# One PSUM pool of single banks, other first loads, and a new order table in an attention-then-FFN kernel

## The chip, the cores and the metric

One core of a Trainium2 chip runs the kernel: TensorE (PE; its weight loads are a row of their own, PEld), VectorE (DVE), ScalarE (ACT), GpSimd (POOL) and SyncE (SP), with 16 DMA engines between the core's SBUF and HBM. PSUM, which PE writes and DVE and ACT read, has eight banks of 128 x 512 float32. The metric is the device time of one execution in microseconds (us); several executions are timed, and their median counts.

## The reference

```
proj = x @ w_phi                                   # q and k: 8 batches, 8 heads, 576 x 64; w_phi 64 x 128
proj = proj - max|proj| over its 128 features
phi  = [exp(proj), exp(-proj)]                     # 256 features
kv = phi(k)^T v;  z = sum over tokens of phi(k)    # per batch and head
attn = phi(q) kv / (phi(q) z + 1e-6)
x = attn, heads side by side                       # 4608 tokens x 512
out = relu(x @ w_in)^2 @ w_out                     # 512 -> 2048 -> 512
```

## The kernel before

The 4608 tokens are 36 tiles of 128. A batch gives two parts of two tiles each and a rest of 64 tokens; the rests of two batches share a tile. The FFN takes the tiles in chunks: four chunks of one tile, then sixteen of two.

**Keys** (`k_batch`). For batches 0 and 1 PE transposes the keys (`e_tp`, line 630) and a copy brings them to SBUF as `kT`; from batch 2 on a DMA transpose does it (`XB_IN` = 2). Then, in five groups, PE multiplies by `w_phi` (`e_kp`, line 660; matmuls on 64 rows, two at a time on the two halves of the array) into a `pj` tile of two PSUM banks. DVE reduces the tile to the largest magnitude per token (`e_red`, line 595, 128x1024), ACT takes exp of +proj and of -proj (`e_exp`, line 602, 128x1024 twice). ACT makes exp of the maxima (`em`, line 704), DVE scales the values by it (`e_va`, line 755; `e_vr`, line 738, for the rest), and PE sums keys times values (`e_kv`, lines 776 and 781, 65 columns a matmul) into what a copy stores as `kvs`.

**Queries** (`q_batch`). Likewise transposed; PE projects twice, with tokens on partitions for the maxima (`e_qm`, line 878) and with features on partitions for the exps (`e_qp`, line 888); DVE reduces (line 925), ACT takes exps (line 915). For each tile PE multiplies the two sign halves with `kvs` (`e_nd`, line 970; line 978 for rests, on half of the columns), DVE scales and adds them (`e_t`, lines 1009 and 1013, 128x520), divides (`e_rd`, `e_xo`, lines 1032 and 1042) and gives the x tile `xo`. For batches 0 and 1 PE transposes `xo` (`e_xtp`, line 1083) and a copy stores `xT`; from batch 2 on (`XB_X` = 2) SP does it by a DMA transpose (lines 1065 and 1068).

**FFN.** `hp_chunk`: 16 matmuls fill one `mo` bank (line 1133), relu to `hr` (lines 1151 on ACT, 1153 on DVE), square into `h` (1161 on ACT, 1163 on DVE, 128x512 each). `op_chunk`: 16 matmuls of 512 columns sum a tile's output in one `mo` bank (line 1189), a copy and an SP DMA bring it out.

**PSUM.** Six banks are three `pj` tiles of two; two banks are `mo`, for transposes, the FFN and batch 0's `kv`.

**Start.** PE runs 24 matmuls on zeros (`e_first`), then waits for the identity that POOL makes after it has issued the loads of half of batch 0's keys and of its values. The other half of the keys comes by SP as float32 and is cast. `WARM` adds idle matmuls ahead of some PE steps, and `e_fill` 40 more in the head. `w2` holds `w_phi` for the two array halves, zeros elsewhere.

**Order.** Every step is an `Op` with the engines that it may run on; the program adds 1718 of them in a fixed sequence, and the table `ORDER` lists their numbers in the order in which they are issued, a minus sign choosing the second engine. Each engine runs its own in that order and waits by semaphores for what it needs. Steps that use the 64-row or half-column form of the array are marked (`mode`), the others use all of it. POOL and SP issue DMAs from their queues, and an issue whose buffer is still in use blocks what is behind it.

Of the kernel before, what the change touches and what calls it, by code (L numbers as in the profile page):

```python
# [8 lines left out]
F32 = mybir.dt.float32  # L9
# [94 lines left out]
)  # L104


WARM = {44: 7, 54: 10, 58: 6, 62: 2, 74: 13, 93: 4, 117: 5, 139: 2, 149: 8}


class Slots:  # L110
# [54 lines left out]
class Plan:  # L165
# [13 lines left out]
    def add(self, key, engines, emit=None, deps=(), take=(), give=(), after=(), locks=(), port=False, mode="full"):  # L179
        op = Op(key, engines, emit, deps, take, give, after, locks, port, mode)  # L180
        self.ops.append(op)
        return op

    def order(self):
        assert sorted(abs(n) for n in ORDER) == list(range(len(self.ops)))
        for n in ORDER:
            o = self.ops[abs(n)]
            assert not o.left
# [1079 lines left out]
```

## Time and profile before

| | |
|---|---|
| median of the runs | 360.28 us (359.89 to 363.01) |
| profiled execution, first to last instruction | 358.4 us |
| the median less that span | 1.9 us |
| first FFN matmul in it | 28.41 us |
| last matmul's end in it | 354.8 us |
| mean granted TensorE clock | 0.990 |

The profile has busy times by engine and by stretches of time, groups of instructions (count, busy us, mean ns of one, idle time ahead of them), a chain of waits that ended last, a timeline (start, duration, instruction, in brackets what ended the idle time) and DMA issues. The profiled execution's own time is taken as its span and the 1.9 us around it.

### The profile page before, as it was taken

To read this page: it belongs to the slowest core of one execution; us is meant where nothing else is said; L and a number is where in the kernel's file an instruction comes from. 1 tells how busy PE (TensorE), PEld (TensorE's weight loads), DVE (VectorE), ACT (ScalarE), POOL (GpSimd) and SP (SyncE) were. 2 spreads that over 40 slices of the span, in tenths; PEclk is the share of its full clock that TensorE was granted. 3 is DMA by queue.
4 is the path that set the end of the run, shared out by engine and by line. 5 is a ranking of instruction groups with operands and counts; after the bars stand their busy time and mean duration, and the time that the engine had idled before them with its cause. 6 is when DMAs were issued, how large, how long until landed. Compare 5 with 4: busy or idle time off the path is not lost.

```text
span 358.4 us, 9254 instructions
## 1 busy us (share of the span) xinstructions
PE 346.4 (97%) x3860; PEld 239.1 (67%) x3894; DVE 292.4 (82%) x529; ACT 262.9 (73%) x436; POOL 58.5 (16%) x88
## 2 busy tenths in 40 slices
PE   8699999999999999999999999999999999999995
PEld 4378667775776676767576757757685768576754
DVE  5979998889998998788988699979988988591310
ACT  4979997996798774698849883798879867544641
POOL 8643323442160113100220002000000000000000
PEclk9969999999999999999999999999999999999999
DMA  9999999999997499607982194435203001113011
GB/s 161 185 197 207 194 208 141 170 181 187 186 152 138 83 171 150 107 15 145 124 126 53 59 149 96 61 89 82 60 16 88 18 35 48 65 34 88 2 59 59
DMA packets 92281, 39.33 MB, mean 110 GB/s; under 512 B 59728, under 2 KB 87760, under 8 KB 92240
## 3 DMA queue, kind: packets, MB, share of 16 engines
q0 software_dynamic: 42752, 18.09, 42.7%
q1 hardware_dynamic: 49328, 20.59, 28.6%
q8 instruction: 30, 0.49, 0.6%
q10 hardware_dynamic: 160, 0.07, 0.1%
q14 instruction: 11, 0.09, 0.1%
HBM read 36.77 MB, written 9.44 MB: 129 GB/s over the span
## 4 chain that ended last, share of the span: by engine, by line
PE 82%; DVE 8%; ACT 7%; issue 1%; POOL 1%; ACTq 0%; POOLq 0%
PE mo L1133 32%; PE mo L1189 31%; PE pj L781 4%; PE pj L970 4%; ACT kph L602 4%; PE pj L878 3%; PE pj L888 2%; DVE m L595 2%; PE pj L660 2%; DVE tmp L1009 1%; ACT hr L1151 1%; PE pj L776 1%; PE mo L781 1%; DVE va L755 1%; DVE hr L1153 1%
## 5 line engine op out<-in xcount | busy, mean ns | idle before, releaser
L1133 PE MATMUL mo<-xT,win 128*128 128x256 bf16 (+1 forms) x1280 | 139.3, 262 | 0.8 <-ACT hr L1151 0.2
L1189 PE MATMUL mo<-wout,h 128*128 128x512 bf16 (+1 forms) x558 | 131.2, 373 | 1.8 <-issue 0.2
L1133 PEld LDWEIGHTS <-win 128*128 128x128 bf16 x1280 | 111.3, 98 | 19.7 <-issue 4.3
L1189 PEld LDWEIGHTS <-h 128*128 128x128 bf16 x592 | 54.5, 98 | 57.3 <-issue 2.8
L915 ACT ACTIVATE qph<-pj 128x1024 bf16<-128x1024 f32 (+1 forms) x80 | 72.8, 940 | 11.6 <-PE pj L888 11.6
L1151 ACT ACTIVATE hr<-mo 128x512 bf16<-128x512 f32 x99 | 58.7, 598 | 28.2 <-PE mo L1133 27.0
L602 ACT ACTIVATE kph<-pj 128x1024 bf16<-128x1024 f32 (+1 forms) x80 | 71.2, 949 | 6.4 <-PE pj L660 4.9
L1163 DVE TENSOR_TENSOR h<-hr 128x512 bf16<-128x512 bf16 x82 | 33.7, 419 | 22.6 <-ACT hr L1151 22.0
L925 DVE TENSOR_REDUCE mq<-pj 128x8 f32<-128x1024 f32 (+1 forms) x40 | 44.2, 1108 | 4.5 <-PE pj L878 4.4
L595 DVE TENSOR_REDUCE m<-pj 128x8 f32<-128x1024 f32 (+1 forms) x40 | 44.3, 1111 | 3.4 <-ACT kph L602 1.7
L1161 ACT ACTIVATE h<-hr 128x512 bf16<-128x512 bf16 x62 | 38.9, 631 | 8.3 <-DVE hr L1153 7.5
L755 DVE TENSOR_TENSOR va<-vin,em 128x512 bf16<-128x512 bf16 x63 | 40.2, 683 | 0.1
L1153 DVE TENSOR_SCALAR hr<-mo 128x512 bf16<-128x512 f32 x45 | 30.6, 684 | 7.9 <-PE mo L1133 7.4
L417 ACT ACTIVATE ot<-mo 128x512 f32<-128x512 f32 (+1 forms) x24 | 14.0, 585 | 25.1 <-PE mo L1189 25.1
L1009 DVE TENSOR_TENSOR tmp<-pj,e 128x520 f32<-128x520 f32 x31 | 21.1, 692 | 6.1 <-PE pj L970 6.1
L970 PEld LDWEIGHTS <-qph 128*128 128x128 bf16 x512 | 21.9, 98 | 5.4 <-issue 1.5
L1042 DVE TENSOR_TENSOR xo<-tmp,rden 128x512 bf16<-128x512 f32 (+1 forms) x39 | 24.3, 631 | 0.5
L970 PE MATMUL pj<-kvs,qph 128*128 128x65 bf16 x512 | 24.4, 194 | 0.2
L781 PEld LDWEIGHTS <-kph 128*128 128x128 bf16 x512 | 21.5, 101 | 0.3
L1013 DVE TENSOR_TENSOR tmp<-pj,tmp 128x520 f32<-128x520 f32 x31 | 21.2, 692 | 0.5 <-PE pj L970 0.4
L781 PE MATMUL pj<-va,kph 128*128 128x65 bf16 x448 | 18.4, 194 | 0.0
L467 POOL DMA_DIRECT2D vin<-in_v_dram x8 | 7.2, 895 | 68.5 <-DVE va L755 63.1
(75 smaller groups left out, 268.5 us busy)
## 6 DMA issues: line engine op xcount, KB each, us to landing
out_dram<-ot SPq DMA_DIRECT2D x31, 256.0 KB, 2.4
vin<-in_v_dram POOLq DMA_DIRECT2D x8, 512.0 KB, 9.0
kin<-in_k_dram POOLq DMA_DIRECT2D x7, 512.0 KB, 11.9
qin<-in_q_dram POOLq DMA_DIRECT2D x7, 512.0 KB, 10.3
win<-in_moe_w_in_dram POOLq DMA_DIRECT2D x4, 512.0 KB, 10.1
wout<-in_moe_w_out_dram POOLq DMA_DIRECT2D x2, 1024.0 KB, 14.8
out_dram<-ot SPq DMA_DIRECT2D x10, 128.0 KB, 2.4
xT<-xo SPq DMA_TRANSPOSE x36, 2.6
```

The source lines that it names most:

```text
L595: nc.vector.tensor_reduce(out=st["m"].rearrange("p (n c) -> p c n", c=2)[:, :, n0 : n0 + n], in_=st["pj", g][:, :, :n], axis=AX.X, op=ALU. ...
L602: nc.scalar.activation(out=st["kph"][:, s, n0 : n0 + n].rearrange("p n c f -> p c n f"), in_=st["pj", g][:, :, :n], func=ACT.Exp, scale=1. ...
L755: nc.vector.tensor_tensor(out=st["va"][:, s, gs, 0:D], in0=tiles["v", b].rearrange("p h i d -> p (h i) d")[:, gs, :], in1=st["em"][:, s, g ...
L781: nc.tensor.matmul(out=kv[:, sum_of(h) - 2 * prs[0], :], lhsT=st["kph"][:, s, 2 * h + i // 2, i % 2, :], rhs=st["va"][:, s, h * NI + i, :] ...
L915: nc.scalar.activation(out=st["qph", pt][:, s, half, n0 : n0 + n], in_=in_, func=ACT.Exp, scale=1.0 - 2.0 * s)
L925: nc.vector.tensor_reduce(out=st["mq", pt][:, half, n0 : n0 + n], in_=in_, axis=AX.X, op=ALU.max, apply_absolute_value=True)
L970: nc.tensor.matmul(out=nps[:, n + 4 * (ab or 0), :], lhsT=qph[:, s, half, sl, :], rhs=kvs[:, s, sum_of(sl), :], start=True, stop=True)
L1133: nc.tensor.matmul(out=hp[:, mi, :], lhsT=win[:, kc, mc * P : (mc + 1) * P], rhs=st_x[c][:, kc, 0:nt, :], start=kc == kcs[0] and (ab is No ...
L1151: nc.scalar.activation(out=out_, in_=in_, func=ACT.Relu)
L1153: nc.vector.tensor_scalar(out=out_, in0=in_, scalar1=0.0, scalar2=None, op0=ALU.max)
L1161: nc.scalar.activation(out=out_, in_=hr, func=ACT.Square)
L1189: nc.tensor.matmul(out=st["op"], lhsT=hst["h2"][:, mc, tt * P : (tt + 1) * P], rhs=wout[:, mc, cols], start=(mc == 0), stop=(mc == KC2 - 1))
```

## The change

PSUM is one ring of eight single banks (`r_ps`). A step that had a two-bank tile takes two banks, each held and given back by itself; so the reduces and exps are two instructions of half the size, numerators come in two steps of four heads, each with two DVE instructions of half the size, and `kv` in two steps of two head pairs for all batches. The lock that keeps DVE and ACT apart on one projection of keys holds per bank. `e_qm` and `e_qp` are separate steps for all batches.

Relu results of two FFN banks lie in one `hr` tile, and one square handles both, except in the last chunk.

Batch 0: SP also loads the rest of the keys, and the values, as float32 in two halves; the rest is cast, the value products read float32. POOL makes the identity first. `w_phi` comes in one transfer to both halves; the zeroing of `w2` is gone. `e_fill` is gone.

POOL may run value products, rest products and `xo`. Only the two x tiles of batch 0's first part go through PE; the other eight of batches 0 and 1 go by SP's DMA transposes. From batch 3 on, the loads of a batch stand behind a small POOL copy that reads an `xo` of two batches earlier. The order table and `WARM` are new: 2084 steps, PE's among them 604 for 502, 47 value and 9 rest products and 21 `xo` with a minus sign (POOL).

```diff
-    XB_IN, XB_X = 2, 2
+    XB_IN, PE_X = 2, [(0, 0, 0), (0, 0, 1)]
...
-    r_pj = Ring("pj", 3, [P, 2, 4, P], F32, pool=ps)
-    r_mo = Ring("mo", 2, [P, 4, P], F32, pool=ps)
+    r_ps = Ring("ps", 8, [P, 4, P], F32, pool=ps)
-    r_hr = Ring("hr", 4, [P, 512], BF16)
+    r_hr = Ring("hr", 3, [P, 2, 512], BF16)
...
-            red_ops[g] = add(key, {"dve": dve(256 * n)}, e_red, [o_kp], give=[(r_pj.slots, hold)], locks=[lock])
+            for par in range(2):
+                lock = Lock()
...
+                red_ops.setdefault(g, []).append(add(key, {"dve": dve(128 * n)}, e_red, [o_kp],
+                                                     give=[(r_ps.slots, holds[par])], locks=[lock]))
...
-            o_fill = fill[0] = add(kd - 5.0, {"pe": (FILL * 0.0565, FILL * 0.0565 + 0.165)}, e_fill, [o_id], [r_mo.slots],
...
-            va_on = {"dve": (0.6, 0.69)}
+            va_on = {"dve": (0.6, 0.69), "pool": (1.0, 1.05)}
...
-                    if b >= XB_X:
+                    if (b, pt, half) not in PE_X:
...
+    def load_gate(b, key):
+        o_xo, owner, st, name = firsts[b - 2]
+
+        def emit(_):
+            nc.gpsimd.tensor_copy(out=mark[:, b : b + 1], in_=st[name][:, 0, 0:1])
```

More of the change, by code (lines that the diff above doesn't have):

```diff
@@ L369, in c_w2 @@
     def c_w2(op):
-        for half in range(2):
-            rows = slice(half * Dh, (half + 1) * Dh)
-            copy(op, w2[rows, half], wst[rows])
+        copy(op, w2, wst)
     def c_wst(_):
-        for half in range(2):
-            nc.scalar.dma_start(out=wst[half * Dh : (half + 1) * Dh], in_=w_phi)
+        nc.scalar.dma_start(out=wst, in_=w_phi.unsqueeze(0).to_broadcast([2, Dh, Fd]))
     def c_var(_):
@@ L417, in copy @@
             nc.scalar.activation(out=out_, in_=in_, func=ACT.Copy)
+        elif op.engine == "pool":
+            nc.gpsimd.tensor_copy(out=out_, in_=in_)
         else:
@@ L453, in load_first_k, with emit_r, e_rcast, emit_v @@
                 casts[g].append(add(-90, either(256), e_cast, [d], give=[(r_h2.slots, o_st)], after=[o_table, o_in]))
-        return casts
-    first_v = []
+        def emit_r(op):
+            st["r"] = r_ot.tile(op, [P, NP, D], [None, 2 * NP, D])
+            for h2 in range(2):
+                nc.sync.dma_start(out=st["r"][h2 * J : (h2 + 1) * J],
+                                  in_=k[0, :, SM:S, :].rearrange("(h2 pr) j d -> h2 j pr d", h2=2)[h2])
+        o_r, d_r = plan.issue("hw", 2, -98, {"sp": (1.0, 1.0)}, emit_r, "krf", (), [r_ot.slots], after=[o])
+        def e_rcast(op):
+            tiles["kr", 0] = r_rest["k"].tile(op)
+            copy(op, tiles["kr", 0], st["r"])
+        o_rc = add(-89, either(256), e_rcast, [d_r], [r_rest["k"].slots], [(r_ot.slots, o_r)], after=[o_table])
+        casts[4] = [o_rc]
+        d_v, o_v, o = [], None, o_r
+        for n in range(2):
+            def emit_v(op, n=n):
+                if n == 0:
+                    tiles["v", 0] = r_h2.tile(op, [P, H, NI, D], dtype=F32)
+                nc.sync.dma_start(out=tiles["v", 0].rearrange("p h i d -> p h (i d)")[:, 4 * n : 4 * n + 4],
+                                  in_=v[0, 4 * n : 4 * n + 4, 0:SM, :].rearrange("h (p i) d -> p h (i d)", i=NI))
+            o, d = plan.issue("hw", 1, -97, {"sp": (0.5, 0.5)}, emit_v, "vf", (), [] if o_v else [r_h2.slots], after=[o])
+            o_v = o_v or o
+            d_v.append(d)
+        return casts, o_rc, o_v, d_v
     def load(name, b, key, after=None):
@@ L481, in main @@
         def main(last):
[L482 removed]
+            return plan.issue("sw", 1, key, {"pool": (0.92, 0.95)}, emit_main, "main", (), [r_in[name].slots],
                               after=[prior, last])
@@ L575, in through_xbar @@
         return x1, t1, t2
-    kv_ops, gate, fill = {}, {}, {}
-    FILL = 40
+    kv_ops, gate = {}, {}
     def k_batch(b):
@@ L640, in e_cp @@
                     copy(op, st["kT"][:, n0 : n0 + n], st["ps", g][:, :n])
-                o_cp = add(key - 1.5, bf_copy(128 * n), e_cp, [o_tp], give=[(r_mo.slots, o_tp)])
+                o_cp = add(key - 1.5, bf_copy(128 * n), e_cp, [o_tp], give=[(r_ps.slots, o_tp)])
             cp_ops[g] = o_cp
         o_kp = None
-        for gs in [[g] for g in groups]:
-            key = kd - 6.0 - 2.2 * (4 - gs[0])
-            holds = {g: Hold(r_pj.slots) for g in gs}
-            def e_kp(op, gs=gs, holds=holds):
-                if gs[0] == 0:
-                    st["kph"], st["m"] = r_kph.tile(op), r_m.tile(op)
-                for g in gs:
-                    n0, n = GROUPS[g]
-                    pj = st["pj", g] = r_pj.tile(holds[g])
-                    warm(pj[:, 0], op.warm if g == gs[0] else 0)
-                    for u in range(n):
-                        for par in range(2):
-                            rows = slice(par * Dh, (par + 1) * Dh)
-                            nc.tensor.matmul(out=pj[:, par, u, :], lhsT=st["kT"][rows, n0 + u, :],
-                                             rhs=w2[rows, par, :], start=True, stop=True)
-            o_kp = add(key - 1, {"pe": mm(P, sum(GROUPS[g][1] for g in gs))}, e_kp,
-                       [cp_ops[g] for g in gs] + [o_w2],
-                       list(holds.values()) + ([r_kph.slots, r_m.slots] if gs[0] == 0 else []),
@@ new lines, in k_batch, with e_kp @@
+        for g in groups:
+            key = kd - 6.0 - 2.2 * (4 - g)
+            holds = [Hold(r_ps.slots) for _ in range(2)]
+            def e_kp(op, g=g, holds=holds):
+                if g == 0:
+                    st["kph"], st["m"] = r_kph.tile(op), r_m.tile(op)
+                n0, n = GROUPS[g]
+                pj = [r_ps.tile(hold) for hold in holds]
+                st["pj", g, 0], st["pj", g, 1] = pj
+                warm(pj[0], op.warm)
+                for u in range(n):
+                    for par in range(2):
+                        rows = slice(par * Dh, (par + 1) * Dh)
+                        nc.tensor.matmul(out=pj[par][:, u, :], lhsT=st["kT"][rows, n0 + u, :], rhs=w2[rows, :],
+                                         start=True, stop=True)
+            o_kp = add(key - 1, {"pe": mm(P, GROUPS[g][1])}, e_kp, [cp_ops[g], o_w2],
+                       holds + ([r_kph.slots, r_m.slots] if g == 0 else []),
@@ L666, in k_batch @@
                        give=[(r_kT.slots, o_kT)], after=[o_k0], mode="row")
             o_k0 = o_k0 or o_kp
[L668 to L679 removed]
+            after_kp(g, o_kp, holds)
@@ L866, in q_batch @@
                 key = xk - 9.0 + (12 if split else 1) * pi
-                hm, hq = Hold(r_pj.slots), Hold(r_pj.slots)
-                size = 256 * w
+                hm, hq = ([Hold(r_ps.slots) for _ in range(2)] for _ in range(2))
+                banks = [(half, 4 * bank, 4) if split else (bank, n0, n) for bank in range(2)]
                 def e_qm(op, pt=pt, pi=pi, mms=mms, w=w, hm=hm):
-                    pj = st["pm", pt, pi] = r_pj.tile(hm)
+                    pj = st["pm", pt, pi] = [r_ps.tile(hold) for hold in hm]
                     if pi == 0:
                         st["mq", pt] = r_mq.tile(op)
-                    warm(pj[:, 0], op.warm)
+                    warm(pj[0], op.warm)
                     for u in range(w):
@@ L877, in e_qm @@
                             rows = slice(par * Dh, (par + 1) * Dh)
-                            nc.tensor.matmul(out=pj[:, bank, u, :], lhsT=q_blocks(st, pt, blk + u, 1)[rows, 0],
-                                             rhs=w2[rows, par, :], start=True, stop=True)
+                            nc.tensor.matmul(out=pj[bank][:, u, :], lhsT=q_blocks(st, pt, blk + u, 1)[rows, 0],
+                                             rhs=w2[rows, :], start=True, stop=True)
                 def e_qp(op, pt=pt, pi=pi, mms=mms, w=w, hq=hq):
-                    pj = st["pq", pt, pi] = r_pj.tile(hq)
+                    pj = st["pq", pt, pi] = [r_ps.tile(hold) for hold in hq]
@@ L907, in q_batch @@
-                if split and pi:
-                    late = o_qm, o_qp
-                o_mq, o_q0 = o_mq or o_qm, o_q0 or o_qp
-                for s in range(2):
-                    def e_exp(op, pt=pt, pi=pi, half=half, n0=n0, n=n, w=w, s=s):
-                        in_ = st["pq", pt, pi][:, :, :w]
-                        if n == 8:
-                            in_ = in_.rearrange("p a b t -> p (a b) t")
-                        nc.scalar.activation(out=st["qph", pt][:, s, half, n0 : n0 + n], in_=in_, func=ACT.Exp,
-                                             scale=1.0 - 2.0 * s)
-                    exps.setdefault(pi, []).append(add(key + 2.5 + 0.2 * s, {"act": act(size)}, e_exp, [o_qp],
-                                                       give=[(r_pj.slots, hq)]))
@@ L921, in e_red @@
-                def e_red(op, pt=pt, pi=pi, half=half, n0=n0, n=n, w=w):
-                    in_ = st["pm", pt, pi][:, :, :w]
-                    if n == 8:
-                        in_ = in_.rearrange("p a b t -> p (a b) t")
-                    nc.vector.tensor_reduce(out=st["mq", pt][:, half, n0 : n0 + n], in_=in_, axis=AX.X, op=ALU.max,
-                                            apply_absolute_value=True)
-                reds.append(add(key + (3.5 if b == 0 else 0.5), {"dve": dve(size)}, e_red, [o_qm], give=[(r_pj.slots, hm)]))
+                o_qm = add(key, {"pe": mm(P, w * (1 + split))}, e_qm, need + [o_w2], hm + first[:1], give=qT_give,
+                           after=[o_mq], mode="row")
@@ new lines, in q_batch, with e_exp, e_red @@
+                o_qp = add(key + (0.1 if b else 2), {"pe": mm(128 * w, 1 + split)}, e_qp, need + [o_w2], hq + first[1:],
+                           give=qT_give, after=[o_q0], mode="row")
+                o_mq, o_q0 = o_mq or o_qm, o_q0 or o_qp
+                mine = []
+                for bank, (half_, h0, nh_) in enumerate(banks):
+                    for s in range(2):
+                        def e_exp(op, pt=pt, pi=pi, bank=bank, half_=half_, h0=h0, nh_=nh_, w=w, s=s):
+                            nc.scalar.activation(out=st["qph", pt][:, s, half_, h0 : h0 + nh_],
+                                                 in_=st["pq", pt, pi][bank][:, :w], func=ACT.Exp, scale=1.0 - 2.0 * s)
+                        exps[half_, h0, s] = add(key + 2.5 + 0.2 * s, {"act": act(128 * w)}, e_exp, [o_qp],
+                                                 give=[(r_ps.slots, hq[bank])])
+                    def e_red(op, pt=pt, pi=pi, bank=bank, half_=half_, h0=h0, nh_=nh_, w=w):
+                        nc.vector.tensor_reduce(out=st["mq", pt][:, half_, h0 : h0 + nh_], in_=st["pm", pt, pi][bank][:, :w],
+                                                axis=AX.X, op=ALU.max, apply_absolute_value=True)
+                    mine.append(add(key + (3.5 if b == 0 else 0.5), {"dve": dve(128 * w)}, e_red, [o_qm],
+                                    give=[(r_ps.slots, hm[bank])]))
@@ new lines, in q_batch @@
+                            give = [(r_ps.slots, hold) for hold in holds]
+                            if s == 0:
+                                give.append((r_e2.slots, e2s[0]))
+                            at = ab or hg
+                            o_t[at] = add(ks - 3.5 + 0.5 * s, {"dve": dve(260) if pt < 2 else (0.85, 0.95)},
+                                          e_t, [o_nd, o_e2, o_t.get(at)], [] if o_tmp else [r_tmp.slots], give=give,
+                                          after=[o_tmp])
@@ L1202, in e_ot @@
                     copy(op, st["ot"], st["op"])
-                o_ot = add(key, either(wide), e_ot, [o_op], [r_ot.slots], give=[(r_mo.slots, first)])
+                o_ot = add(key, either(wide), e_ot, [o_op], [r_ot.slots], give=[(r_ps.slots, first)])
                 def e_out(op, st=st, tt=tt, cols=cols):
```

316 lines of the change are left out of this document (147 added, 169 removed), and 190 rows, old and new, of the table ORDER.

## The prediction

> **What bounds the kernel now.** I read the page's busy shares first, then the busy time by stretches, the chain of waits, the groups of instructions, and last the timeline of the first 30 us.
>
> ```profile
> span 358.4 us, 9254 instructions
> PE 346.4 (97%) x3860; PEld 239.1 (67%) x3894; DVE 292.4 (82%) x529; ACT 262.9 (73%) x436; POOL 58.5 (16%) x88
> 0.00:10.00 10.00, 8.26 (x63) 4.09 (x64) 6.08 (x11) 4.86 (x8) 8.01 (x16) 1.00 1.11 158
> 10.00:20.00 10.00, 6.73 (x66) 4.15 (x65) 9.72 (x19) 10.00 (x27) 6.18 (x11) 0.84 1.37 193
> 20.00:30.00 10.00, 9.82 (x154) 8.07 (x154) 8.21 (x18) 7.01 (x12) 5.66 (x8) 0.82 1.39 199
> 30.00:110.00 80.00, 78.42 (x1033) 55.41 (x1040) 73.88 (x134) 68.64 (x116) 25.88 (x37) 1.00 1.44 180
> ```
>
> The last four rows are stretches: length, then busy us and count for PE, PEld, DVE, ACT and POOL, the granted clock, the DMA share and GB/s. PE is busy nearly always, but a matmul's row lasts longer than its turn in the stream, so the share hides small gaps. In 10 to 20 us ACT is full; from 30 to 110 us DVE is busy 92% and ACT 86%. What PE needs at its own rate comes from these rows, of the chain (start, length, what), of the groups and of the timeline:
>
> ```profile
> 326.87 10.51 PE mo L1133 x96
> 339.99 5.18 PE mo L1189 x24
> 311.48 0.73 PE pj L970 x24
> 348.09 6.69 PE mo L1189 x46
> L1133 PE MATMUL mo<-xT,win 128*128 128x256 bf16 x1024 | 123.2, 273 | 0.4 <-ACT hr L1151 0.2
> L1133 PE MATMUL mo<-xT,win 128*128 128x128 bf16 x256 | 16.1, 219 | 0.4 <-ACT kT L417 0.2
> L1189 PEld LDWEIGHTS <-h 128*128 128x128 bf16 x592 | 54.5, 98 | 57.3 <-issue 2.8
> 28.41 1.96 PE L1133 MATMUL mo<-xT,win 128*128 128x128 bf16 x32
> ```
>
> 96 matmuls of 256 columns in 10.51 us are 109 ns each; 24 of 512 in 5.18 are 216; 24 of 65 in 0.73 are 30; 32 of 128 in 1.96, less the last one's 219 ns, are 56. The FFN is then 1024 x 0.109 + 256 x 0.056 + 560 x 0.216 + 32 x 0.109 (592 weight loads; the last tile's 32 are 256 wide) = 250 us. The attention by the program's counts: 1024 of 65 columns and 64 of 130 (two steps) 35, 288 pairs of 64-row matmuls 16, 40 wider pairs 8, 64 half-column pairs 2, 108 transposes 6: 67 us. Sum 317 us, 89% of the span. What is left: the first FFN matmul starts at 28.41 us, with only some 8 us of PE work ahead of it, so 20 us are lost at the head; the last matmul ends at 348.09 + 6.69 = 354.8, so 3.6 us of tail; between, 326.4 us hold 309 us of work, so 17 are lost. PE bounds the kernel after the head; the head is bound by ACT and by a chain of dependent steps.
>
> **The change, part by part.** The sum goes against the profiled execution, span 358.4 us; the median of the runs shown, 360.28, is 1.9 us more.
>
> *Head.* Rows of its timeline:
>
> ```profile
> 4.34 0.93 PE L396 MATMUL mo<-ident 128*128 128x128 bf16 x7 [0.61 <-POOL ident masks.py:199]
> 6.67 0.40 PE L660 MATMUL pj<-w,kT 64*128 64x128 bf16 x8
> 7.11 1.23 DVE L595 TENSOR_REDUCE m<-pj 128x8 f32<-128x1024 f32 x1 [0.75 <-PE pj L660]
> 8.36 2.85 ACT L602 ACTIVATE kph<-pj 128x1024 bf16<-128x1024 f32 x3 [0.34 <-DVE m L595]
> 9.07 2.33 PE L400 MATMUL mo<-ident 128*128 128x512 bf16 x10
> 16.66 0.93 PE L878 MATMUL pj<-w,qT 64*128 64x128 bf16 x8 [1.97 <-DVE m L595]
> 18.84 0.65 PE L781 MATMUL mo<-va,kph 128*128 128x65 bf16 x8
> 23.97 0.41 PE L781 MATMUL mo<-va,kph 128*128 128x65 bf16 x8
> 24.72 0.39 ACT L417 ACTIVATE kvs<-mo 128x260 bf16<-128x260 f32 x1 [0.88 <-PE mo L781]
> ```
>
> PE waits 0.61 us for the identity; POOL making it first saves up to 1 us of the start. The first exp waits for the whole reduce (8.36 behind 7.11 + 1.23); with a lock per bank, the exp of one bank starts beside the reduce of the other, so at about 7.11 - 1.0 = 6.1, 2.2 us earlier. But ACT has more to do. In the new table it runs, from there to the last key exp of batch 0, 20 key exps (16 of 512 at 0.60 us, 4 of 256 at 0.39, as the copy of 260) and 8 query exps of 512, and about 2 us of small work: 18 us, to 24.1. From the end of the last `kvs` copy (25.1) to the first FFN matmul are 3.3 us now; with a last `kv` and copy (0.8) the new one starts at 24.1 + 0.8 + 3.3 = 28.2. Against that, more is done by then: three groups of batch 1's key transposes (12 x 0.056 = 0.7 us) and part of a second tile's numerators. I take -1.2 us; bounds -4 (ACT's copy and exps at their back-to-back pace, and the 2 us PE wait at 16.66 gone, since eight banks come free singly) to +2.5 (the later key exps delay the last sums). `e_fill` (2.33 us at 9.07) lay in a wait, so it is worth 0 by itself. The float32 loads go to SP's queue, which has nothing else until the first output, and leave POOL's; the cast of the key rest (one DVE copy, below 0.3 us) and one w_phi transfer less are within the bounds.
>
> About the clock: matmuls of 65 columns ran 0.65 us for eight at 18.84 and 0.41 at 23.97, and the granted clock was 0.84 and 0.82 in these stretches, behind PE's pauses. The Trainium skill (TensorE: Matmul & The Clock Gate, Part 1) says that a window of about 3.4 us without work halves the clock until PE has been busy for another; the trace agrees in kind. By that rule, the lost fill could cost another cold window: about 1.7 us, an estimate from the page, and the sum would be 355.2.
>
> *PSUM in single banks, squares over two banks.* Prices, by form:
>
> ```profile
> L915 ACT ACTIVATE qph<-pj 128x1024 bf16<-128x1024 f32 x64 | 63.5, 1025 | 11.6 <-PE pj L888 11.6
> L915 ACT ACTIVATE qph<-pj 128x512 bf16<-128x512 f32 x16 | 9.4, 600 | 0.0
> L595 DVE TENSOR_REDUCE m<-pj 128x8 f32<-128x1024 f32 x32 | 38.8, 1218 | 3.4 <-ACT kph L602 1.7 <-PE pj L660 1.2
> L595 DVE TENSOR_REDUCE m<-pj 128x4 f32<-128x512 f32 x8 | 5.5, 683 | 0.1
> L1009 DVE TENSOR_TENSOR tmp<-pj,e 128x520 f32<-128x520 f32 x31 | 21.1, 692 | 6.1 <-PE pj L970 6.1
> L1001 DVE TENSOR_TENSOR tmp<-pj,e 128x260 f32<-128x260 f32 x2 | 0.8, 422 | 0.6 <-PE pj L970 0.6
> L1163 DVE TENSOR_TENSOR h<-hr 128x512 bf16<-128x512 bf16 x82 | 33.7, 419 | 22.6 <-ACT hr L1151 22.0
> L1161 ACT ACTIVATE h<-hr 128x512 bf16<-128x512 bf16 x62 | 38.9, 631 | 8.3 <-DVE hr L1153 7.5
> L755 DVE TENSOR_TENSOR va<-vin,em 128x512 bf16<-128x512 bf16 x63 | 40.2, 683 | 0.1
> masks.py:199 POOL TENSOR_SCALAR_AFFINE_SELECT ident<-ident 128x128 bf16<-128x128 bf16 x1 | 0.3, 287 | 0.1
> ```
>
> An exp of 1024 becomes two of 512: 2 x 600 - 1025 = +0.175 us, for 128 of them +22; the 32 of 512 likewise +0.175, +6. A reduce gains 2 x 683 - 1218 = 0.15 us: 64 of them +10, the 16 small ones +2. The numerators: 2 x 422 - 692 = 0.15, 62 times, +9. A double square saves about 0.18 us (the fixed part: 512 elements more cost DVE 0.27, ACT 0.43), 68 times: -12. 77 products leave DVE at 0.68 each: -53. Eight copies of x tiles go: -4. So ACT and DVE together have 292.4 + 262.9 + 28 + 12 + 9 - 12 - 53 - 4 = 535 us for 555: 75% of two engines over 355 us. Neither becomes the bound, and the stretch from 30 to 110 us gets air. The value is in PE's waits: now an output sum holds one of two `mo` banks for 16 x 0.216 = 3.5 us.
>
> *POOL.* It has no product in this trace. Bounds: DVE's 0.68 us, and four times its own 128x128 select, 1.15 us. I take 1.15, its own engine's row: 77 x 1.15 = 89 us on 58.5, 41% busy. The eight value products of batch 0 then take 9.2 us; with the values landed at about 12 us they end at 21, ahead of ACT's 24. So 0, covered by ACT's exps; without the cover each 0.1 us per product costs 0.8. The load gate puts the loads of a batch, and the products listed behind it, behind an `xo`; the loads have some 40 us until they are used, and PE has FFN work: 0.
>
> *x tiles by transfers.* 28 transposes of 128 columns leave PE at 56 ns: -1.6 us. SP issues 10 transfers of about 1.2 us more. Their time to landing:
>
> ```profile
> L1065 SPq DMA_TRANSPOSE xT<-xo x24: 1189/1216/2124, 103.6 to 323.9; - x24
> DMA to landing us min/median/max: 2.3/2.6/7.6
> L566 SPq DMA_TRANSPOSE kT<-kin x6: 1332/4031/6397, 51.8 to 207.3; - x6
> DMA to landing us min/median/max: 2.3/5.9/12.8
> ```
>
> The first two rows are the x tiles' (issue in ns, all after 103 us; then to landing), the last two the key transposes' (from 52 us on, where the DMA share is 1.44). PE has 6 to 9 us of other steps in the table between such a transfer and the chunk that needs it. I take 6 us to landing, the median of the rows in that stretch, and 0; bounds 0 and 10 us.
>
> *Array forms.* Where PE goes from 128-row to 64-row matmuls and back it pauses:
>
> ```profile
> 188.71 2.78 PE L1133 MATMUL mo<-xT,win 128*128 128x256 bf16 x24
> 191.42 0.73 PE L660 MATMUL pj<-w,kT 64*128 64x128 bf16 x20
> 192.09 1.05 PE L1133 MATMUL mo<-xT,win 128*128 128x256 bf16 x8
> ```
>
> 24 x 0.109 = 2.62, but the next starts 2.71 after: 0.1; ten pairs x 0.056 = 0.56 take 0.67: 0.1 again. Walking both tables step by step, I count 112 changes of form from the first FFN matmul on before, and 87 in the new one: -25 x 0.1 = -2.5 us. 112 x 0.1 = 11 of the 17 us lost; some 6 are left as waits. Of these I take -1.5, for the eight banks; bounds -5 (nearly all) and +6 (the finer steps and new waits double them).
>
> Sum: 358.4 - 1.2 - 1.6 - 2.5 - 1.5 = 351.6; with the 1.9 around it 353.5 us.
>
> **The rivals.** *Late x tiles (slower).* The transfers of batches 0 and 1 land after 12.8 us, as the slowest key transpose did, in place of 6: chunks 2 to 6 each wait 12.8 - 8 = 5 us less what other steps fill, say 3 to 4. Five times that is 15 to 20 us, less the gain of 6.8: 369 to 373, or 364 to 369 when three or four chunks are hit. It decides from 6.8 us of such waits on. For it: the DMA share of 1.44 up to 110 us. Against it: the new gate thins the loads there, and these transfers are small.
>
> *The products hold the sums (no change).* POOL at three times DVE's 0.68, 2 us a product, which no row excludes: batch 0's end at 12 + 16 = 28 us, +4 on the head, and 1 to 2 us more in batch 1: 359. The Trainium skill (GPSIMD Engine Reference, section 4.1) speaks for this side: two-input products about twice DVE's time, so 1.37 us, an estimate; and section 1, an SBUF interface shared with DVE. No run here shows either yet. At 1.37 batch 0's end at 23 and the sum stays.
>
> *The split does not free PE (no change).* If DVE and ACT, not the bank count, end the waits between 30 and 110 us, the last term is 0 or positive; with the head at +2.5 the sum is 358.4 + 2.5 - 1.6 - 2.5 + 1.5 + 1.9 = 360.2.
>
> **How the numbers follow.** The forecast has 0.70, with 347 to 357 as its own range (head at -4 and waits at -5 give 347.2; head at +2.5, waits at 0, 358.7, cut where the next case begins); the two cases without change 0.08 and 0.06; late tiles 0.16. Within 1% (about what a measurement of this kernel can tell from no change) is 356.7 to 363.9. So faster 0.70, same 0.14, slower 0.16. The range is 347 to 361: it takes the forecast's and the cases without change, and leaves out the late tiles.
>
> **What would show it.** Right: the first FFN matmul at 26 to 28.5 us; first exp near 6 us; 28 fewer transposes on PE, most in 40 to 105 us, the x tiles landing within 8 us there; POOL's products near 1.15 us; the last matmul's end near 348; PE's lost time in between down by 4 us. Wrong: FFN matmuls that wait for a DMA of `xT`, or `kv` that waits for POOL; either beyond 7 us in sum turns the sign. Also wrong: a head above 31 us.

## The result, and the profile after

The changed kernel takes 387.88 us (median, 385.19 to 388.58), the kernel before 360.08 beside it: 1.074 times as long, interval 1.070 to 1.079. The prediction was 353.5 us, faster. Its profiled execution spans 386.8 us.

The page's first lines:

```profile
span 386.8 us, 9506 instructions
PE 355.2 (92%) x3850; PEld 242.9 (63%) x3850; DVE 282.7 (73%) x574; ACT 254.6 (66%) x548; POOL 140.1 (36%) x165
```

The busy times by stretches, same columns as before the change:

```profile
0.00:10.00 10.00, 6.42 (x37) 2.94 (x38) 4.59 (x9) 4.69 (x9) 8.98 (x17) 1.00 0.88 184
10.00:20.00 10.00, 7.45 (x57) 4.01 (x58) 8.47 (x17) 6.73 (x21) 4.30 (x5) 1.00 1.42 208
20.00:30.00 10.00, 9.26 (x102) 6.26 (x97) 7.69 (x14) 6.03 (x15) 9.83 (x11) 1.00 1.16 164
30.00:110.00 80.00, 70.89 (x973) 52.54 (x971) 66.86 (x142) 61.11 (x139) 33.87 (x41) 0.96 1.09 131
110.00:260.00 150.00, 138.69 (x1495) 92.42 (x1493) 116.95 (x231) 106.99 (x232) 59.42 (x70) 0.98 0.73 108
```

The kernel before in the last stretch:

```profile
110.00:260.00 150.00, 148.89 (x1612) 101.49 (x1626) 134.61 (x239) 113.39 (x181) 12.77 (x18) 1.00 0.59 99
```

PE was idle 1.6 us from 30 to 110 us and is now idle 9.1; from 110 to 260 it was 1.1 and is 11.3. DVE and ACT are *less* busy, together 537 us (535 was predicted; that it came out is in part luck, since exps of 613 and 627 ns for 600 add 5 us and slower products of DVE 4): neither became the bound, PE waits. The list of PE's waits (what waited, for what; sum, times, longest) and the rows around the longest one, of PE, SP and POOL:

```profile
PE ps L1141 <- DMA xT<-xo: 8.8, 6, 3.1
PE ps L1141 <- issue: 6.2, 1, 6.2
PE ps L798 <- DVE var L762: 1.7, 3, 0.7
PE ps L1141 <- DVE tmp L1019: 1.1, 2, 0.6
```

```profile
77.09 0.30 PE L977 MATMUL ps<-kvs,qph 128*128 128x65 bf16 x4
83.63 1.65 PE L1141 MATMUL ps<-xT,win 128*128 128x256 bf16 x7 [6.24 <-issue]
74.81 1.22 SPq L1073 DMA_TRANSPOSE xT<-xo  x1
76.82 7.52 SPq L606 DMA_TRANSPOSE qT<-qin  x1
73.69 1.04 POOL L1047 TENSOR_TENSOR xo<-tmp,rden 128x512 bf16<-128x512 f32 x1 [0.75 <-DVE rden L1037]
74.67 0.95 POOL L510 DMA_DIRECT2D kin<-in_k_dram  x1
75.61 1.25 POOL L520 DMA_DIRECT2D krest<-in_k_dram  x2
76.83 0.92 POOL L510 DMA_DIRECT2D qin<-in_q_dram  x1
```

Chunk 4 starts at 83.63. The "issue" wait is one for a transfer too: the last x tile's, issued at 74.81. It lands 8.7 us later, while the fastest takes 2.3, in this row of its line (the tiles of the parts):

```profile
L1073 SPq DMA_TRANSPOSE xT<-xo x30: 1189/1190/2150, 45.6 to 359.9; - x30
DMA to landing us min/median/max: 2.3/2.5/8.7
```

POOL releases it and a burst of loads in the same microsecond, since the `xo` stands ahead of the loads on its queue. A like picture comes back at 150 us: the gate's copy, behind an `xo` of DVE, lets loads go from 151.2 us on, and PE waits 3.1 and 1.8 us for x tiles. The head, and the prices of the new forms:

```profile
5.85 0.31 ACT L433 ACTIVATE w<-wst 128x128 bf16<-128x128 f32 x1 [1.90 <-DMA wst<-in_w_phi_dram]
9.36 0.61 PE L698 MATMUL ps<-w,kT 64*128 64x128 bf16 x8 [1.25 <-DVE kT L437]
21.49 2.73 DVE L762 TENSOR_TENSOR var<-vrest,em 64x512 bf16<-64x512 bf16 x2
34.04 1.16 PE L1141 MATMUL ps<-xT,win 128*128 128x128 bf16 x18
```

```profile
L641 ACT ACTIVATE kph<-ps 128x512 bf16<-128x512 f32 x128 | 71.3, 627 | 7.9 <-PE ps L698 6.1 <-DVE m L633 1.3
L633 DVE TENSOR_REDUCE m<-ps 128x4 f32<-128x512 f32 x64 | 42.2, 682 | 9.2 <-PE ps L698 5.4 <-ACT kph L641 3.6
L780 POOL TENSOR_TENSOR va<-vin,em 128x512 bf16<-128x512 bf16 x39 | 44.1, 1157 | 37.4 <-ACT em L729 34.9 <-issue 2.2
L780 DVE TENSOR_TENSOR va<-vin,em 128x512 bf16<-128x512 bf16 x17 | 15.6, 928 | 0.7 <-issue 0.4 <-ACT em L729 0.3
```

The prices of the reduce and of POOL came as predicted (682 and 1157 ns), that of ACT's exp close to it (627 for 600). The row not foreseen is the last: DVE's own product, 683 ns before, takes 928 in the mean. Eleven of the 17 still take 0.68 to 0.70 us. The other six began while a product of POOL ran; they take 0.99 to 1.58 us, and each ends 0.55 or 0.56 us behind POOL's. The first FFN matmul is 5.6 us late (34.04 for 28.41).

### The profile page after: what moved, and what is told of

Same layout as the page of the kernel before. It is cut to its first block, busy times and chain, and to the rows that moved or that the text cites. A ratio compares the mean times of both kernels' runs of the same rounds, so it can differ in the third digit from the quotient of the medians.

```text
span 386.8 us, 9506 instructions
## 1 busy us (share of the span) xinstructions
PE 355.2 (92%) x3850; PEld 242.9 (63%) x3850; DVE 282.7 (73%) x574; ACT 254.6 (66%) x548; POOL 140.1 (36%) x165
## 4 chain that ended last, share of the span: by engine, by line
PE 58%; DVE 20%; DMA 9%; ACT 6%; issue 4%; POOL 1%; SPq 1%; DVEq 0%; ACTq 0%
PE ps L1141 24%; PE ps L1212 22%; DMA xT<-xo 7%; PE ps L977 3%; DVE mq L928 3%; ACT kph L641 3%; PE ps L698 2%; PE ps L803 2%; DVE hr L1169 2%; DVE tmp L1012 2%; DVE var L762 2%; DVE m L633 2%; DMA ot<-in_k_dram 2%; DVE h L1185 2%; DVE xo L1047 1%
## 5 line engine op out<-in xcount | busy, mean ns | idle before, releaser
L1141 PE MATMUL ps<-xT,win 128*128 128x256 bf16 (+1 forms) x1280 | 141.2, 266 | 17.1 <-DMA xT<-xo 8.8
L1212 PE MATMUL ps<-wout,h 128*128 128x512 bf16 (+1 forms) x592 | 135.7, 374 | 0.6 <-ACT h L1183 0.3
L1212 PEld LDWEIGHTS <-h 128*128 128x128 bf16 x592 | 54.0, 98 | 54.6 <-ACT h L1183 1.2
L921 ACT ACTIVATE qph<-ps 128x512 bf16<-128x512 f32 (+1 forms) x160 | 80.0, 570 | 10.6 <-PE ps L907 10.3
L641 ACT ACTIVATE kph<-ps 128x512 bf16<-128x512 f32 (+1 forms) x160 | 79.3, 584 | 8.7 <-PE ps L698 6.1
L1167 ACT ACTIVATE hr<-ps 128x512 bf16<-128x512 f32 x83 | 48.6, 604 | 43.4 <-PE ps L1141 35.3
L1169 DVE TENSOR_SCALAR hr<-ps 128x512 bf16<-128x512 f32 x61 | 41.3, 682 | 34.7 <-PE ps L1141 34.3
L780 POOL TENSOR_TENSOR va<-vin,em 128x512 bf16<-128x512 bf16 x39 | 44.1, 1157 | 37.4 <-ACT em L729 34.9
L633 DVE TENSOR_REDUCE m<-ps 128x4 f32<-128x512 f32 (+1 forms) x80 | 48.0, 629 | 10.6 <-PE ps L698 6.9
L928 DVE TENSOR_REDUCE mq<-ps 128x4 f32<-128x512 f32 (+1 forms) x80 | 47.8, 626 | 6.1 <-PE ps L897 5.7
L1183 ACT ACTIVATE h<-hr 128x1024 bf16<-128x1024 bf16 (+1 forms) x35 | 35.5, 1025 | 18.1 <-DVE hr L1169 15.2
```

The costliest lines, as they stand in the source:

```text
L633: nc.vector.tensor_reduce(out=st["m"].rearrange("p (n c) -> p c n", c=2)[:, par, n0 : n0 + n], in_=st["pj", g, par][:, :n], axis=AX.X, op= ...
L641: nc.scalar.activation(out=st["kph"][:, s, n0 : n0 + n, par, :], in_=st["pj", g, par][:, :n], func=ACT.Exp, scale=1.0 - 2.0 * s)
L780: eng.tensor_tensor(out=st["va"][:, s, gs, 0:D], in0=tiles["v", b].rearrange("p h i d -> p (h i) d")[:, gs, :], in1=st["em"][:, s, gs].uns ...
L921: nc.scalar.activation(out=st["qph", pt][:, s, half_, h0 : h0 + nh_], in_=st["pq", pt, pi][bank][:, :w], func=ACT.Exp, scale=1.0 - 2.0 * s)
L928: nc.vector.tensor_reduce(out=st["mq", pt][:, half_, h0 : h0 + nh_], in_=st["pm", pt, pi][bank][:, :w], axis=AX.X, op=ALU.max, apply_absol ...
L1141: nc.tensor.matmul(out=hp[:, mi, :], lhsT=win[:, kc, mc * P : (mc + 1) * P], rhs=st_x[c][:, kc, 0:nt, :], start=kc == kcs[0] and (ab is No ...
```

## The experiments

Theory 1: bursts of loads make the x transfers late. Theory 2: the eight new transfers are the loss, whatever the loads. Theory 3: POOL's products slow DVE. The first four runs undo or do one part alone.

**x tiles through PE again (changed kernel).**

```diff
-    XB_IN, PE_X = 2, [(0, 0, 0), (0, 0, 1)]
+    XB_IN, PE_X = 2, [(b_, pt_, h_) for b_ in (0, 1) for pt_ in (0, 1, 2) for h_ in (0, 1)]
```

> The changed kernel with the other eight x tiles of batches 0 and 1 through PE and a copy again, as before the change; loads, POOL products and banks stay. Theory 1 (transfers are late where they meet a burst of loads which the gate and POOL's products release at once): the 6.4 us wait ahead of chunk 4 and the cold clock behind it go, some 10 us, but the waits at 154, 158, 202 and 240 us stay, since those tiles go by transfer in both kernels: 375 to 379 us. Theory 2 (all of the loss is the eight new transfers): 362 us or less. Theory 3 (POOL's products slow DVE and ACT, the transfers only show it): 385 to 388.

Measured 383.26 us, ratio to before 1.065 (1.062 to 1.068): 4.6 us back, between the figures of theories 1 and 3, and far from theory 2's. The wait ahead of chunk 4 goes; others come up, two of them (1.0 and 1.6 us) at the new transposes, and 5.6 us of waits for other x tiles stay.

**Loads as early as buffers allow (changed kernel).** In the table the loads of batches 3 to 7 move behind the previous load of the same input.

```diff
-            nc.gpsimd.tensor_copy(out=mark[:, b : b + 1], in_=st[name][:, 0, 0:1])
+            nc.gpsimd.memset(mark[:, b : b + 1], 0.0)
...
-        return add(key, {"pool": (0.1, 0.12)}, emit, [o_xo], give=[(r_xo.slots, owner)])
+        return add(key, {"pool": (0.1, 0.12)}, emit)
```

> The changed kernel with the loads of batches 3 to 7 issued as soon as a buffer is free, as before the change: the gate's copy no longer reads an x tile, and the loads are listed right behind the previous load of the same input. The x tiles stay transfers. Theory 1: the x tiles land in 2.5 to 4 us nearly everywhere, the 18 us of waits for them and 3 us of cold clock shrink to under 5: 366 to 372 us. Theory 2: loads earlier meet the new transfers of the first 110 us even more, 385 to 395. Theory 3: 385 to 388.

Measured 396.48 us, 1.102 (1.099 to 1.105): slower still. PE waits 11.7 us for x tiles, once for 7.0, and 5.3 more ahead of chunk 4, which the list puts down to ACT (PE starts at 88.5, when the x tile issued at 81.3 has landed, 7.1 us later). Loads issued sooner meet other x tiles, so this run speaks against theory 1 as far as *earlier* was its cure.

**xo on DVE (changed kernel).** The 21 minus signs of `xo` in the table go.

> The changed kernel with all xo products on DVE (21 leave POOL); value products stay on POOL. Theory 1: the xo are ready some 0.5 us sooner and the loads listed behind them no longer wait for DVE's work: the bursts move, 378 to 386. Theory 3: a third of POOL's load beside DVE goes, 378 to 382, spread over the whole span and not at single waits.

Measured 400.04 us, 1.110 (1.106 to 1.114). A miss for both theories: in a table made for POOL's `xo`, DVE gets to them late, and the x tiles leave later: the one issued at 74.8 us in the changed kernel leaves at 78.2 and takes 9.2 us to land.

**The transfers alone, in the kernel before.** The same line as in the first diff, the other way round, in place of `XB_X`; each transfer is listed right behind its `xo`.

> The kernel before with one part of the change alone: the x tiles of batches 0 and 1, all but the first two, by transfers; two-bank tiles, loads and products as before. Theory 1: its loads run ahead and are spread, but there are loads at 68 to 73 us too; one or two chunks wait 2 to 4 us: 361 to 367. Theory 2: the transfers alone cost 10 us or more: 370 to 375. If transfers are hidden: 358 to 360.

Measured 380.50 us, 1.056 (1.053 to 1.059): 20 us from this part alone, more than theory 2's 370 to 375. But it is mostly one wait, ahead of chunk 4. PE's list of waits:

```profile
PE mo L1131 <- DMA xT<-xo: 20.4, 3, 17.8
```

SP's queue, and one of DVE's rows, in the timeline:

```profile
67.06 0.68 DVE L1040 TENSOR_TENSOR xo<-tmp,rden 128x512 bf16<-128x512 f32 x1
70.64 7.49 SPq L564 DMA_TRANSPOSE kT<-kin  x1
78.22 1.92 SPq L1063 DMA_TRANSPOSE xT<-xo  x1
```

The tile is ready at 67.7 us. Its transfer is issued at 78.2, behind a key transpose whose issue holds SP's queue for 7.49 us, with two more transfers of the chunk at 81.6 behind it, and they land 7 to 8 us after their issue, among loads; chunk 4 starts at 89.6.

**The same, with that key transpose behind the x transfers.** One entry of the table moves.

> The kernel before with the eight x tiles by transfers, as in the run that took 380.5 us, and the key transpose of batch 3 moved behind the x transfers of chunk 4 on SP's queue. There the transfer of the last x tile stood 7.5 us behind that transpose and then took 9.5 us to land. If the queue is the cost, the wait of 18 us ahead of chunk 4 falls to 8 to 11 us and the time to 370 to 373; if the time to landing is, the wait stays at 16 to 18 and the time at 378 to 381.

PE's list of waits:

```profile
PE mo L1131 <- DMA xT<-xo: 12.0, 5, 9.9
```

Measured 372.44 us, 1.036 (1.030 to 1.041). As the queue theory said: 8 us of the wait were the queue. Of the other 10, 7.0 are the time from the issue of the last x tile (75.8) to its landing.

**Main loads cut to an eighth, in both kernels.** The tiles of batches 3 to 7 are not allocated anew, so that they keep old values, and the output is another one.

```diff
...
+                nh = 1 if b >= 3 else H
-                nc.gpsimd.dma_start(out=tiles[name, b].rearrange("p h i d -> p h (i d)"),
+                nc.gpsimd.dma_start(out=tiles[name, b].rearrange("p h i d -> p h (i d)")[:, 0:nh],
...
```

> The changed kernel with the main loads of batches 3 to 7 cut to one head of eight (their tiles keep what the batch two before left there, so the output is another one); every instruction, wait and place in the table stays. If loads that the gate and POOL's queue release in bursts make the x transfers late (theory 1), the transfers land in 2.3 to 3 us from 75 us on, the 16 us of PE's waits for x tiles fall to under 4 and the time to 368 to 374 us. If the waits have another cause (xo late, SP's queue, DVE and ACT), 382 to 388.

> The kernel before with the same cut of its loads of batches 3 to 7: the control. Its PE waits 1.5 us in all behind the first FFN matmul, so both theories expect 357 to 361 us; less would show that the bytes cost something beside waits.

Changed kernel: 377.86 us, 1.048 (1.041 to 1.055), 10 us back, less than the 14 to 20 that theory 1 gave; the kernel before 360.30, 1.001 (0.999 to 1.003), nothing. The transfer that chunk 4 waits for, issued at 74.8 us, with the cut:

```profile
L1076 SPq DMA_TRANSPOSE xT<-xo x1: 2031/2031/2031, 74.8 to 74.8; - x1
DMA to landing us min/median/max: 4.7/4.7/4.7
```

It took 8.7 us. The rests have a line of their own; their transfers in the changed kernel, then with the cut:

```profile
L1076 SPq DMA_TRANSPOSE xT<-xo x16: 1161/1238/2369, 69.1 to 329.6; - x16
DMA to landing us min/median/max: 2.3/3.2/7.7
L1079 SPq DMA_TRANSPOSE xT<-xo x16: 1160/1227/2075, 69.1 to 319.7; - x16
DMA to landing us min/median/max: 2.3/3.1/4.0
```

PE's list of waits with the cut:

```profile
PE ps L1144 <- DMA xT<-xo: 4.7, 5, 1.7
PE ps L1144 <- ACT kph L644: 2.2, 1, 2.2
```

The second row is the wait ahead of chunk 4, which ends at 79.55, when the tile issued at 74.8 has landed. So 15 us of waits for x tiles became 6.9, which is 8 of the 10 us. Theory 1 is right in its mechanism and a third of the loss.

**The gate's wait alone** (the memset of the diff above, the table as it is).

> The changed kernel with the load gate's copy turned into a memset that waits for nothing; its place in the table, and that of the loads, stays. If the gate's wait for an x tile lines the loads up with that tile's transfer (theory 1 in its narrow form), the loads of batches 3 and 5 are issued 1 to 4 us sooner, the transfers at 75 and 150 us land in 3 to 5 us in place of 7 to 9, and the time falls by 5 to 10 us. If POOL's queue is held by its products and by places in the table, whatever the gate does: 385 to 389.

Measured 388.38 us, 1.079 (1.074 to 1.084). The narrow form of theory 1 falls: the burst comes sooner (at 150 us by 5.7 us) and meets the same x tiles. With the run of small loads, it is the bytes behind POOL's place in the table, not the gate.

**The head: w_phi and the key rest's cast.** In the table the cast moves one place later.

```diff
-        nc.scalar.dma_start(out=wst, in_=w_phi.unsqueeze(0).to_broadcast([2, Dh, Fd]))
+        for half in range(2):
+            nc.scalar.dma_start(out=wst[half * Dh : (half + 1) * Dh], in_=w_phi)
```

> The changed kernel with w_phi in two transfers as before the change, and DVE's cast of the key rest one place later, behind the copy of the second group's transposes. If these two set the head (first FFN matmul at 34.04 us, 5.6 later than before the change), PE's second projection comes at about 7.9 in place of 9.36 us, the first at about 5.7 in place of 6.21, and the first FFN matmul at 32 to 32.6; the time falls by 1.4 to 2 us. If DVE beside POOL's products sets it (casts of 0.6 us for 0.3, rest products of 1.36 for 0.69, between 16 and 24 us), the first FFN matmul stays at 33.5 or later.

**The head: more warm-up.**

```diff
-WARM = {47: 2, 57: 3, 64: 7, 78: 2, 85: 13, 138: 8, 148: 6, 110: 6, 246: 3}
+WARM = {47: 2, 57: 14, 64: 19, 78: 4, 85: 13, 134: 4, 136: 10, 138: 14, 148: 6, 110: 12, 246: 6}
```

> The changed kernel with more warm-up matmuls ahead of the steps where PE waits in the head (the order stays). If PE's half clock in the head (eight steps of 128 columns in 0.61 us for 0.40) is part of the 5.6 us, PE's steps there shorten by a third and the first FFN matmul comes at 32 to 33 us, the time 1 to 2 us lower; if the head hangs on ACT, DVE and POOL, no change within 0.5 us.

First: 385.96 us, 1.073 (1.070 to 1.076), first FFN matmul at 32.86. Second: 384.90, 1.070 (1.065 to 1.075), at 31.71. Both intervals overlap the changed kernel's, and runs with an untouched head had that matmul at 32.5 to 34.1, so the first edit is not told from nothing. The second is, in the profile: the step that took 0.61 us takes 0.40. What it gives the head is 0.8 to 2.4 us against those runs.

```profile
9.12 0.40 PE L696 MATMUL ps<-w,kT 64*128 64x128 bf16 x8 [0.82 <-DVE kT L435]
```

Its 2.3 us are gone by chunk 4, which starts at 83.07 for 83.63: there the late x tile sets the time, and an earlier PE waits longer (8.0 us for 6.2).

**Four suspects at once** (x tiles, both head edits, small loads).

> The changed kernel with four suspects undone together: the eight x tiles through PE, w_phi and the key rest's cast as in the head experiment, more warm-up matmuls, and the main loads of batches 3 to 7 cut to an eighth (another output). If the parts add (10 us for the loads, 2 for the other x tiles once those are cut, 3 for the head), 371 to 373 us. What then remains over 360 is the products on POOL, the single banks and the table. If the parts overlap (a wait removed shows the next one), 375 to 378; if x tiles, loads and head are all of it, 360 to 364.

Measured 373.11 us, 1.036 (1.033 to 1.040): nearly the sum. 13 us stay, with the first FFN matmul at 31.31. DVE's rows ahead of batch 0's sums in this run, and POOL's first eight products beside them:

```profile
15.00 2.03 DVE L436 CAST var<-em 64x8 bf16<-64x8 f32 x2
19.40 3.04 DVE L766 TENSOR_TENSOR var<-vrest,em 64x512 bf16<-64x512 bf16 x2
12.93 4.06 POOL L784 TENSOR_TENSOR va<-h,em 128x512 bf16<-128x512 f32 x4 [2.98 <-ACT em L733]
18.40 4.95 POOL L784 TENSOR_TENSOR va<-h,em 128x512 bf16<-128x512 f32 x4 [1.41 <-ACT em L733]
```

**POOL beside DVE, in the kernel before.** Each value product of batches 1 to 7 is made once more by POOL, into a spare tile.

```diff
...
+                            nc.gpsimd.tensor_tensor(
+                                out=spare, in0=ident[:, 0:D].unsqueeze(1).to_broadcast([P, 8, D]),
+                                in1=st["em"][:, s, gs].unsqueeze(2).to_broadcast([P, 8, D]), op=ALU.mult)
```

> The kernel before, in which POOL makes, beside each value product of DVE of batches 1 to 7, a product of the same size into a spare tile (56 of about 1.1 us; the output stays). It doubles the suspected contention and delays the loads that stand behind a product, with everything else as before. If POOL beside DVE is costly, DVE's value products go from 683 to 900 ns and more, DVE from 82% to over 86%, and the time to 366 to 375 us. If it only costs POOL's own time, 359 to 362.

Measured 414.80 us, 1.151 (1.147 to 1.156): 54.6 us from work that nobody reads, far above the 366 to 375 expected. DVE is busy 44 us more (336.7 for 292.4), and PE's longest waits, 6.8, 6.6 and 5.9 us, are for DVE. DVE's groups in it (the first was 683 ns, the second 692):

```profile
L754 DVE TENSOR_TENSOR va<-vin,em 128x512 bf16<-128x512 bf16 x63 | 60.2, 1001 | 0.1
L1016 DVE TENSOR_TENSOR tmp<-pj,tmp 128x520 f32<-128x520 f32 x31 | 21.2, 694 | 0.5 <-PE pj L973 0.4
```

All products of DVE, and those of POOL (shortest, median, longest in ns; first and last start):

```profile
L754 DVE TENSOR_TENSOR va<-vin,em x63: 643/690/2384, 12.7 to 348.7; 128x512 bf16<-128x512 bf16 x63
L759 POOL TENSOR_TENSOR spare<-ident,em x56: 1037/1367/1655, 43.7 to 344.1; 128x512 bf16<-128x512 bf16 x56
```

DVE's products that overlap none of POOL's (35) take 0.68 us in the middle, the 28 that do 1.53, and up to 2.38; sums of PSUM keep 694 ns. Of the 28, 23 began while a product of POOL ran, and each ends 0.55 or 0.56 us behind POOL's, as here (51.97 for 51.42):

```profile
50.38 1.04 POOL L759 TENSOR_TENSOR spare<-ident,em 128x512 bf16<-128x512 bf16 x1
50.59 1.38 DVE L754 TENSOR_TENSOR va<-vin,em 128x512 bf16<-128x512 bf16 x1
```

**POOL's products cut to 8 of 64 columns** (value and rest products from batch 1 on, `xo` from batch 2 on), alone and on top of the four.

```diff
...
+                        w = 8 if b and op.engine == "pool" else D
-                            out=st["va"][:, s, gs, 0:D],
+                            out=st["va"][:, s, gs, 0:w],
...
```

> The changed kernel with POOL's products cut to 8 of 64 columns: value products from batch 1 on, rest products from batch 1 on, xo from batch 2 on (the rest of those tiles keeps old values: another output). Instructions, waits and table stay; the loads stay whole. If POOL beside DVE carries the remaining 13 us, the time falls to 372 to 378 and DVE's value products come back to about 690 ns. If the products were only idle time of POOL: 385 to 389.

> The same cut of POOL's products on top of the kernel with x tiles through PE, head mended and loads cut (373.1 us). If the products are the rest of the loss: 360 to 364 us. If the single banks and the table are: 370 to 373. In between, the shares.

Alone 384.35 us, 1.068 (1.062 to 1.073), not told from the changed kernel and far from the 372 to 378 of one theory; on top 367.83, 1.022 (1.018 to 1.026), where 373.11 stood: 5.3 us. The cut shortens POOL's own work too, so this is the price of both. In the first of the two, DVE's product is back at 701 ns.

**A fill in the kernel before.** A step for PE's wait of 1.97 us ahead of the first query projection:

```diff
+    o_f2 = add(0, {"pe": (1.7, 1.9)}, lambda op: warm(r_mo.tile(op), 24), [o_id], [r_mo.slots])
```

> The kernel before with 24 more warm-up matmuls in PE's wait of 1.97 us ahead of the first query projection (at 14.7 us). If the half clock between 16.7 and 23.9 us (eight steps of 65 columns in 0.65 us) sets the head, those steps take 0.41 us and the first FFN matmul comes 0.5 to 2 us sooner than 28.4, the time 358 to 359.5 us. If ACT sets the head: no difference.

```profile
17.74 0.41 PE L780 MATMUL mo<-va,kph 128*128 128x65 bf16 x8
26.31 0.90 PE L1132 MATMUL mo<-xT,win 128*128 128x128 bf16 x13
```

Measured 358.60 us, 0.996 (0.994 to 0.9985): 1.6 us less than the kernel before, small but clear of the spread. The 65-column steps take 0.41 us for 0.65, and the first FFN matmul comes at 26.31.

## Why the prediction was wrong

The 27.8 us, in the order in which they were taken away: 387.9, with small loads 377.9 (-10.0), with x tiles through PE and the head mended 373.1 (-4.8), with POOL's products cut 367.8 (-5.3), against 360.1: 7.7 stay. The shares hang on the order, since waits hide one another. Both signs that the prediction named for being wrong came: waits for x tiles of 15 us, and a head above 31.

*x tiles by transfers, "6 us to landing, and 0"* is the step that failed most. "PE has 6 to 9 us of other steps" did not hold in the run: behind the issue of the last x tile of chunk 4 (74.81) PE had 2.6 us of them until it waited (at 77.39), and ahead of most other waits for x tiles 2.0 to 5.4. Nor is the cost the median landing: chunk 4 needs the latest of its tiles, and that one met a burst (8.7 us). What was left of the 8.7 us is the wait of 6.2; even the 6 us taken would have left 3.4. The transfers by themselves cost the kernel before 20 us, 8 of them on SP's queue, of which the prediction counted the ten issues of 1.2 us and not the 7.5 us issue of a key transpose that stands ahead. The rival *late x tiles* had the mechanism, and 0.16; its 15 to 20 us of waits came near the 15 measured, but 8 of these lie behind 150 us and not at the chunks that it named, and its 364 to 373 us lack the head's loss and DVE's.

*The load gate, "0"*: its wait is worth 0, as the run without it shows. What it should have been priced by is when the loads land: they moved later (the last is issued at 259.7 us, before the change at 222.1) and into bursts, and their bytes cost 10 us. "The new gate thins the loads there" held in the mean, where the DMA share from 30 to 110 us fell from 1.44 to 1.09, and did not help: one burst behind the `xo` was enough.

*POOL, "1.15 us a product"*: the price held (1.157), its neighbour's was left out: the shared interface that one rival named became a reason for slower products of POOL alone. DVE's 17 products go from 683 to 928 ns in the mean, and in the doubled run those that meet POOL's to 1.5 us. The Trainium skill (SBUF — State Buffer, SBUF: two separate sides) says that a DVE instruction with two SBUF inputs and a GpSimd one that reads SBUF exclude each other for the whole instruction. The trace agrees for the 23 products of the doubled run that began while one of POOL's ran: they end 0.55 us behind it, and the sums of PSUM did not change. DVE's longest, 2.38 us, does not fit: it began 0.76 us ahead of the product of POOL that it met (1.06 us), and still ended 0.56 us behind it. "The products hold the sums" gave 359; it priced POOL's time and not DVE's. Batch 0's eight ended at 25.1 us for the predicted 21.

*Head, "-1.2"*: +5.6, outside its bounds of -4 to +2.5. The figure does not follow from its own working, which gives 28.2 us and 0.7 more for the added steps, or +0.5. Two parts of the loss are PE at half rate, 0.8 to 2.4 us, and the late w_phi and cast, 0 to 1.2. The first exp came at 6.86 for the predicted 6.1, since the one w_phi transfer landed at 5.8. That the other 2.9 us (31.31 to 28.41) are the two casts and two products of DVE slowed by POOL is argued from their rows (5.07 us, where four such took 1.8 before), not shown by a run.

*`e_fill`, "0 by itself"*, and the clock: by the rule of the Trainium skill (TensorE: Matmul & The Clock Gate, Part 1), a window of about 3.4 us without work that halves the clock, the sum would have been 1.7 us higher, an estimate from the page. The trace agrees with the lower rate: more warm-up made the same steps 0.40 us for 0.61 here, and 0.41 for 0.65 in the kernel before. It does not show that 3.4 us without work are needed: in the kernel before, eight 64-row matmuls take 0.40 us at 12.38 and 0.93 at 16.66, and the longest pause between them is 1.97. The granted clock did not show the lower rate: 1.00 in the stretches up to 20 us, in which the changed kernel's steps took 0.61 us.

*Waits, "-1.5"*: against 22 us more behind the first FFN matmul (27.8 less the head's 5.6), 18 of them PE's idle time from 30 to 260 us. There was little for eight banks to free: before, PE was idle 2.7 us in those stretches. What the rest of the 6 us that were "left as waits" was, no run shows.

*Form changes, "-2.5"*, and the prices of the split forms: the reduces and numerators held, the exps cost 13 and 27 ns more; no run isolates the changes of form.

What stays open: the last 7.7 us, of which 2.8 lie in the head. The rest is mostly PE waiting 0.2 to 1.6 us at a time for ACT and DVE; that this is an order made for other times is argued, not shown. Single banks and order table could not be taken apart, since the old table has no entries for single banks.

## What to carry to other kernels

When a tile moves from an engine to a DMA queue, price the latest of the tiles that one consumer needs: what stands ahead of it on the issuing queue, and which loads are released in the same microsecond. Work moved to POOL is not free for DVE even where POOL is idle, if both read SBUF; price the neighbour's instructions too. Where PE is bound, a pause behind which its steps run slower is worth filling: here one pause of 1.97 us was worth 1.6 us.

## What was not expected of the hardware

The issue of a whole batch's DMA transpose holds SP's queue for 1.3 us at the least in the kernel before, for 7.5 us at 76.8 in the changed kernel, where loads run beside it, and for 4.2 there with the loads cut; what stands behind it is issued later. A cast of DVE with a single SBUF input suffered too beside POOL. The kernel before:

```profile
L716 DVE CAST va<-em 128x64 bf16<-128x64 f32 x6 | 1.8, 303 | 0.0
```

The same with POOL's doubled products:

```profile
L715 DVE CAST va<-em 128x64 bf16<-128x64 f32 x6 | 7.5, 1256 | 0.0
```
